# One PSUM read per engine for the transposed softmax weights of a query tile, kept in one tile per unit

## The chip, the cores and the metric

The kernel runs on one core of one Trainium2 chip. The metric is the device time of the whole program, in microseconds (us), as a median over several runs. Three runs of the kernel before gave 2176.07, 2176.35 and 2176.68 us.

## The reference, cut to what matters

The program computes sliding-window attention, then a feed-forward layer with a squared ReLU, then a dense mixture of eight experts with a Sinkhorn-normalised gate. Only the attention is touched:

```
B, H, S, D = 4, 8, 576, 64          # window 128
scores = scale * q @ k.T ; bias by distance ; masked outside 0 <= i - j < 128
attn = softmax(scores) ; attn_out = attn @ v
x = attn_out as (B*S, H*D) = (2304, 512)      # input of the feed-forward layer
```

With a window of 128, a tile of 128 queries sees at most two blocks of 128 keys: its own and the one before it.

## The kernel before

**Units.** The attention is cut into 32 units: four batches, two parts of a batch ("early": the query tiles 0, 1 and 2; "rest": the query tile 3 and a tail of 64 queries, numbered 4), and four pairs of heads. A unit loads k, q and v, transposes k and q on TensorE, and then works through its query tiles. Matmuls run on pairs of fp32r numbers: each operand is held as a rounded part (hi) and the remainder (lo), and a product is three matmuls, hi with hi, hi with lo and lo with hi. `split_ps` (L112) makes such a pair out of a PSUM tile: ScalarE (ACT) rounds PSUM into hi, then VectorE (DVE) subtracts hi from the same PSUM tile into lo.

**One query tile.** `attention_scores` (L257) computes the scores of two heads, the bias and the maximum, the exponential, the sum and the scaling, into the tile `s`. `attention_weights` (L302) transposes `s` with TensorE into one PSUM bank `pt` (L322: two heads by one or two key blocks, 128x128 each) and calls `split_ps` on it. Where a query tile has two key blocks, it calls it twice: first for the half of `pt` that belongs to the key block before, which goes into the second half of that block's tiles, then for the half of its own key block, which goes into the first half of new tiles. So there is one pair of tiles `p0`, `p1` for each key block, holding [head, own or next query tile, 128 queries]; three buffers of each stand in the pool (`weights`, L254). `attention_values` (L350) then multiplies by v: at query tile 1 it issues `block` (L327) for key block 0, at query tile 2 for key blocks 1 and 2, and in a rest unit, at the tail, for 3, 2 and 4. `block` is six matmuls into the PSUM tile `xo` (L336), whose first needs hi and whose second needs lo. `put_x` evicts `xo` into the input of the feed-forward layer.

**Order of the work.** `plan` (L375) lists steps: "q" for the transposes of k and q of a unit, "s" for the scores of a query tile, "t" for its weights and values. In the first four units two units alternate and "t" runs two steps behind "s"; after that one step behind. Before each of the five chunks of tokens of the feed-forward layer, `advance(needed(...))` makes sure that the attention of this chunk is done (L675), and inside a chunk `part` hands out the steps of the next chunk at three points of each of the 16 turns: after the first matmuls (h), in the middle of the second ones (acc), and at the end of the turn. The first chunk (384 tokens) also converts all weights from pairs of 32-bit words (`narrow`, L434: ACT L440 and L442, DVE L443, L444, L447 and L451, then the split in L453 and L454). Up to L720 the framework arranges each engine's queue: it takes the instructions in the order of the program, but lets a later one pass an earlier one that, by its own model of durations, isn't ready yet. From L720 on, the order of the program is kept.

Of the kernel before, what the change touches and what calls it, by code (L numbers as in the profile page):

```python
# [9 lines left out]
F32R = mybir.dt.float32r  # L10
# [13 lines left out]
def raw(ap):  # L24

    return ap.bitcast(F32)
# [3 lines left out]
def attention_moe_moe2(  # L30
# [12 lines left out]
    nc = tc.nc  # L43
    P = 128
# [7 lines left out]
    TAIL = S - FULL * P  # L52
# [26 lines left out]
    def chunk(c):  # L79
        return starts[c], widths[c]  # L80
# [13 lines left out]
    ident = const.tile([P, P], F32, name="ident")  # L94
# [17 lines left out]
    def split_ps(ps, hi, lo):  # L112
        nc.scalar.activation(hi, ps, AF.Copy)
        nc.vector.tensor_sub(lo, ps, raw(hi))
# [24 lines left out]
    ap = att.enter_context(tc.tile_pool(name="ap", bufs=1, side="right"))  # L139
# [22 lines left out]
    def at_ps(name, t, many=early):  # L162
        pool, tag = many[psn[0] % len(many)] if t["alone"] else (ps_at, "at")
        psn[0] += 1
        return pool.tile([P, 512], F32, name=name, tag=tag)
# [10 lines left out]
    def tails_ready():  # L176

        for i in range(SETS):
            for n in range(2):
                nc.scalar.activation(qtail[i][n].rearrange("p j c -> p (j c)"), ones, AF.Copy, scale=0.0)  # L180
        for hp in range(NPAIR):
            for j in range(2):
                nc.scalar.copy(
                    tbias[j * TAIL : (j + 1) * TAIL, hp, :], bias[0:TAIL, 2 * hp + j, : P + TAIL]
                )
# [19 lines left out]
    def attention_qk(n, t):  # L205

        rest = t["rest"]
        hi, lo = {}, {}
        for nm in "kq":
            hi[nm] = ap.tile([P, EARLY], F32R, name=f"{nm}h", tag=f"{nm}h", bufs=2)  # L210
            lo[nm] = ap.tile([P, EARLY], F32R, name=f"{nm}l", tag=f"{nm}l", bufs=2)
            t[nm + "h"], t[nm + "l"] = hi[nm], lo[nm]

        def turn(ps, nm, blocks, tail):
            o = 0
            for c in range(blocks + tail):
                rows = TAIL if c == blocks else P
                nc.tensor.transpose(
                    ps[:, o : o + rows], t[nm][:rows, c].rearrange("p j d -> p (j d)"), ident[:rows, :rows]
                )  # L220
                o += rows
            return ps[:, :o]

        if not rest:
            ps = turn(at_ps("tp_k", t), "k", 3, 0)
            split_ps(ps, hi["k"], lo["k"])
            ps = turn(at_ps("tp_q", t), "q", 3, 0)
            split_q(ps, hi["q"], lo["q"])
        else:
            both = at_ps("tp", t)  # L230
            ps = turn(both, "k", 2, 1)
            w = 2 * P + TAIL
            split_ps(ps, hi["k"][:, :w], lo["k"][:, :w])
            ps = turn(both[:, w:], "q", 1, 1)
            split_q(ps[:, :P], hi["q"][:, :P], lo["q"][:, :P])
            t["qt"] = qtail[n % SETS]
            for j in range(2):
                r = slice(j * D, (j + 1) * D)
                split_q(ps[r, P:], *[x[r, j, :] for x in t["qt"]])

    def attention_v(n, t):

        rest = t["rest"]
        vh, vl = t["vs"] = vsplit[n % SETS]
        cuts = [(slice(0, P), slice(0, 2)), (slice(0, TAIL), slice(2, 3))] if rest else [(slice(0, P), slice(0, 3))]
        for rows, ts in cuts:
            nc.scalar.activation(vh[rows, ts, ::2], t["v"][rows, ts], AF.Copy)
            nc.gpsimd.tensor_sub(vl[rows, ts, ::2], t["v"][rows, ts], raw(vh[rows, ts, ::2]))
# [3 lines left out]
        nc.vector.scalar_tensor_tensor(lo, ps, -(D ** -0.5), raw(hi), op0=ALU.mult, op1=ALU.subtract)  # L252

    def weights():  # L254
        return [ap.tile([P, 2, 2, P], F32R, name=f"p{n}", tag=f"p{n}", bufs=3) for n in range(2)]

    def attention_scores(hp, t, i):  # L257

# [43 lines left out]
    def attention_weights(t, i):  # L302

        s, tail, blocks = t[i], i == FULL, 2 if i else 1

        p = t["p"][i] = weights()
        if i and i - 1 not in t["p"]:
            t["p"][i - 1] = weights()
        pt = at_ps("pt", t)
        if tail:  # L310
            prev = t["p"][i - 1]
            for kb in range(2):
                nc.tensor.transpose(pt[:, kb * P : (kb + 1) * P], s[:, 0, kb * P : (kb + 1) * P], ident)
            pv = pt[:, :P].rearrange("p (j c) -> p j c", j=2)
            split_ps(pv, *[x[:, :, 1, :TAIL] for x in prev])
            pv = pt[:TAIL, P : 2 * P].rearrange("p (j c) -> p j c", j=2)
            split_ps(pv, *[x[:TAIL, :, 0, :TAIL] for x in p])
            return
        pv = pt.rearrange("p (a j c) -> p a j c", a=2, j=2)
        for j in range(2):  # L320
            for kb in range(blocks):
                nc.tensor.transpose(pv[:, kb, j, :], s[:, j, kb * P : (kb + 1) * P], ident)  # L322
        if i:
            split_ps(pv[:, 0], *[x[:, :, 1, :] for x in t["p"][i - 1]])
        split_ps(pv[:, blocks - 1], *[x[:, :, 0, :] for x in p])

    def block(t, kb, dst, a, w, first, last):  # L327

        rows = TAIL if kb == FULL else P
        vs = [x[:rows, kb - (2 if t["rest"] else 0)].rearrange("p a d -> p (a d)") for x in t["vs"]]  # L330
        n = 0
        for j in range(2):
            lh, ll = [x[:, j * D : j * D + P] for x in vs]
            rh, rl = [x[:rows, j].rearrange("p a c -> p (a c)")[:, a : a + w] for x in t["p"][kb]]
            for l, r in ((lh, rh), (lh, rl), (ll, rh)):
                nc.tensor.matmul(  # L336
                    dst, lhsT=l, rhs=r, start=first and n == 0, stop=last and n == 5, skip_group_check=True
                )
                n += 1
# [10 lines left out]
    def attention_values(b, hp, t, i):  # L350

        if i == 1:
            xo = t["xo"] = at_ps("xo", t, [xo_early[hp % 2]])
            block(t, 0, xo[:, : 2 * P], 0, 2 * P, True, False)
        if i == 2:
            xo = t["xo"]
            block(t, 1, xo[:, P : 3 * P], 0, 2 * P, False, False)
            block(t, 2, xo[:, 2 * P : 3 * P], 0, P, False, True)
            put_x(xo, hp, b * S, EARLY)
        if i == FULL:  # L360
            xo = at_ps("xo", t)
            block(t, 3, xo[:, : P + TAIL], 0, P + TAIL, True, False)
            block(t, 2, xo[:, :P], P, P, False, False)
            block(t, 4, xo[:, P : P + TAIL], 0, TAIL, False, True)
            put_x(xo, hp, b * S + EARLY, P + TAIL)
# [3 lines left out]
    ts = {}  # L369

    def load(n):
        if n < len(units):
            ts[n] = attention_load(*units[n])
# [33 lines left out]
    def advance(n):  # L407
        for kind, m, i in steps[done[0] : n]:
            b, hp, rest = units[m]
            if kind == "q":  # L410
                if m == NPAIR:
                    tails_ready()
                attention_qk(m, ts[m])
                ts[m]["p"] = {}
            elif kind == "s":
                attention_scores(hp, ts[m], i)
                if i in (1, FULL):
                    attention_v(m, ts[m])
                    load(m + 2)
            else:  # L420
                attention_weights(ts[m], i)
                attention_values(b, hp, ts[m], i)
        done[0] = max(done[0], n)
# [228 lines left out]
    def part(i):  # L652

        c, f = now
        if c < NCH - 1:
            a, b = [needed(starts[x] + widths[x]) for x in (c, c + 1)]
            advance(a + (b - a) * (3 * f + i) // (3 * NF1))
# [9 lines left out]
    for c in range(NCH):  # L667
        c0, n = chunk(c)
        if c == 1:
            cvs.close()  # L670
            xp2 = m1.enter_context(tc.tile_pool(name="xp2", bufs=1))
            for i in range(3, NCH):
                new_x(xp2, i)

        advance(needed(c0 + n))  # L675
        if c == NCH - 1:
            att.close()
# [6 lines left out]
        for f in range(NF1):  # L684
            now[:] = c, f
            a, bw = ahead.pop(0)
# [4 lines left out]
            hp, tag = (ps_mm, "mm") if c < NCH - 1 else (ps_at, "at")  # L691
# [14 lines left out]
            if len(pending) > LAG:  # L706
                t = pending.pop(0)
# [296 lines left out]
    for n in range(NP):  # L1004
        if n == 0:
# [16 lines left out]
            rh, rl = [x[:, 0, :HALF] for x in hidden[0]]  # L1022
# [243 lines left out]
```

## Time and profile before

| what | us |
|---|---|
| median of three runs | 2176.35 |
| span of the profiled execution | 2174.1 |
| median less the profiled span | 2.25 |
| DVE busy in 62 to 200 us of the span | 129.94 of 138 |
| PE busy in 200 to 602 us of the span | 397.88 of 402 |

Times inside the span are counted from its first instruction. PE is TensorE's matmul queue and PEld its queue of weight loads, which overlaps it. In a timeline row the first number is the start, the second the time taken, and the bracket says how long the engine had been idle and what released it. Instructions of one engine can overlap: a start can come before the end of the one in front. PEclk is the granted clock of TensorE as a share of full speed. The attention lies in the first 602 us; the experts fill the time from about 690 us on.

### The profile page before, as it was taken

What the parts mean: (1) busy time and instruction counts of PE and PEld (TensorE: products, weight loads), DVE (VectorE), ACT (ScalarE), POOL (GpSimd) and SP (SyncE); (2) the same over time, 40 slices, a digit from 0 to 9 for tenths busy, and PEclk for the clock granted to TensorE, in tenths of its full rate; (3) what the DMA queues carried; (4) which work ended last, traced back from release to release, by engine and by line L of the source; (5) the groups of instructions that cost most, each with busy time, mean ns of one, the idle gap of its engine ahead of it and who ended that gap; (6) DMA issues with size and microseconds to landing.
All of it is one profiled execution on the core that took longest, in us unless ns stands there. A gap on an engine that the chain in (4) does not pass through costs nothing.

```text
span 2174.1 us, 32629 instructions
## 1 busy us (share of the span) xinstructions
PE 2103.4 (97%) x11360; PEld 1925.0 (89%) x11360; DVE 1490.4 (69%) x2667; ACT 996.3 (46%) x2050; POOL 1070.5 (49%) x709
## 2 busy tenths in 40 slices
PE   6889999999999899999999999999999999999998
PEld 4778777777888788899999899999999999999998
DVE  7998455453244788887788677666778567777666
ACT  6776445443333444444444444444444544444443
POOL 2222223123254777788888544444546445454442
PEclk9899999999999999999999999999999999999999
DMA  6776545445475877687888988777777877778773
GB/s 186 219 246 209 148 148 162 143 148 177 157 259 170 300 276 294 263 331 284 320 287 299 333 275 265 260 260 260 259 260 265 271 260 252 253 258 269 259 260 125
DMA packets 281730, 525.49 MB, mean 242 GB/s; under 512 B 85584, under 2 KB 129760, under 8 KB 277472
## 3 DMA queue, kind: packets, MB, share of 16 engines
q1 hardware_dynamic: 281568, 523.42, 71.5%
q8 instruction: 91, 1.49, 0.3%
q14 instruction: 71, 0.58, 0.1%
HBM read 379.60 MB, written 143.73 MB: 241 GB/s over the span
## 4 chain that ended last, share of the span: by engine, by line
PE 77%; DVE 12%; ACT 3%; DMA 3%; issue 2%; POOL 1%; SPq 1%; ACTq 0%; POOLq 0%; DVEq 0%
PE y L119 9%; PE y L120 9%; PE y L118 9%; PE g L118 9%; PE g L120 9%; PE g L119 9%; PE h L118 3%; PE acc L118 3%; PE h L120 3%; PE h L119 3%; PE xo L336 3%; PE acc L120 3%; PE acc L119 2%; PE sc L282 2%; DVE rl L936 1%
## 5 line engine op out<-in xcount | busy, mean ns | idle before, releaser
L1086 POOL TENSOR_TENSOR rb<-R,rb 128x768 fp32r<-128x768 f32 x95 | 212.3, 2235 | 334.7 <-ACT rb L1081 322.3
L1117 DVE TENSOR_TENSOR a<-y,a 128x384 f32<-128x384 f32 x434 | 240.0, 554 | 180.0 <-PE y L120 178.0
L1086 POOL TENSOR_TENSOR rt<-R,rt 128x768 fp32r<-128x768 f32 x125 | 238.8, 1922 | 146.3 <-issue 61.7
L110 POOL TENSOR_TENSOR gl<-r,gh 128x512 fp32r<-128x512 f32 (+1 forms) x80 | 99.0, 1237 | 355.1 <-ACT gh L109 336.1
L110 POOL TENSOR_TENSOR w2a<-r,w2a 128x1024 fp32r<-128x1024 f32 x64 | 155.2, 2425 | 67.1 <-ACT w2a L109 67.1
L1081 ACT ACTIVATE rt<-R 128x768 fp32r<-128x768 f32 x128 | 107.7, 842 | 148.5 <-DVE R L1068 90.1
L118 PE MATMUL g<-xt,w1o 128*128 128x384 f32 x512 | 173.0, 338 | 0.9 <-ACT u L809 0.6
L120 PE MATMUL g<-xt,w1o 128*128 128x384 f32 x512 | 172.6, 337 | 0.0
L118 PE MATMUL y<-rt,w2o 128*128 128x384 f32 x512 | 172.4, 337 | 0.1
L120 PE MATMUL y<-rt,w2o 128*128 128x384 f32 x512 | 172.5, 337 | 0.0
L119 PE MATMUL g<-xt,w1o 128*128 128x384 f32 x512 | 172.4, 337 | 0.0
L119 PE MATMUL y<-rt,w2o 128*128 128x384 f32 x512 | 172.1, 336 | 0.0
L118 PE MATMUL y<-w2a,rh 128*128 128x512 f32 x384 | 151.1, 394 | 0.0
L119 PE MATMUL y<-w2a,rh 128*128 128x512 f32 x384 | 150.9, 393 | 0.2 <-POOL w2a L110 0.2
L120 PE MATMUL y<-w2a,rl 128*128 128x512 f32 x384 | 150.2, 391 | 0.0
L698 DVE SCALAR_TENSOR_TENSOR r<-h,r 128x512 f32<-128x512 f32 (+1 forms) x80 | 50.9, 636 | 134.5 <-ACT r L696 134.5
L1063 DVE TENSOR_TENSOR R<-R,pb 128x768 f32<-128x768 f32 x128 | 137.8, 1078 | 5.2 <-ACT R L1176 3.0
L118 PE MATMUL y<-rb,w2o 128*128 128x384 f32 x384 | 129.9, 338 | 2.8 <-DVE a L1117 2.1
L119 PE MATMUL y<-rb,w2o 128*128 128x384 f32 x384 | 130.0, 339 | 2.3 <-POOL rb L1086 2.3
L120 PE MATMUL y<-rb,w2o 128*128 128x384 f32 x384 | 129.9, 338 | 0.0
L120 PE MATMUL g<-xb,w1o 128*128 128x384 f32 x384 | 129.2, 336 | 0.0
L118 PE MATMUL g<-xb,w1o 128*128 128x384 f32 x384 | 129.1, 336 | 0.0
(231 smaller groups left out, 6234.4 us busy)
## 6 DMA issues: line engine op xcount, KB each, us to landing
w1o<-d_w SPq DMA_DIRECT2D x448, 256.0 KB, 3.1
w2o<-d_w SPq DMA_DIRECT2D x224, 512.0 KB, 4.0
d_w<-w1a SPq DMA_DIRECT2D x32, 1792.0 KB, 11.7
d_w<-w2a SPq DMA_DIRECT2D x32, 1536.0 KB, 8.1
a<-d_in SPq DMA_DIRECT2D x64, 512.0 KB, 3.8
b<-d_out SPq DMA_DIRECT2D x64, 512.0 KB, 3.6
r<-in_moe_w_dram SPq DMA_DIRECT2D x64, 512.0 KB, 4.3
u<-in_moe_w_in_dram SPq DMA_DIRECT2D x16, 512.0 KB, 4.6
```

Of the source, the lines that this page charges most:

```text
L110: (eng or nc.gpsimd).tensor_sub(lo, src, raw(hi))
L118: nc.tensor.matmul(ps, lhsT=lh, rhs=rh, start=first, stop=False, **kw)
L119: nc.tensor.matmul(ps, lhsT=lh, rhs=rl, start=False, stop=False, **kw)
L120: nc.tensor.matmul(ps, lhsT=ll, rhs=rh, start=False, stop=last, **kw)
L282: nc.tensor.matmul(sc[:, :nk], lhsT=lhs, rhs=rhs, start=x == 0, stop=x == 2)
L336: nc.tensor.matmul(dst, lhsT=l, rhs=r, start=first and n == 0, stop=last and n == 5, skip_group_check=True)
L698: nc.vector.scalar_tensor_tensor(g[:, :n], ph[:, :n], 0.0, r[:, :n], op0=ALU.max, op1=ALU.mult)
L936: nc.vector.scalar_tensor_tensor(rl, src, 0.0, raw(rh), op0=ALU.max, op1=ALU.subtract)
L1063: nc.vector.tensor_mul(r, r, pb[:, None, :].to_broadcast([P, 2, HALF]))
L1081: nc.scalar.activation(x[:, 0], R[m, f, h], AF.Copy)
L1086: eng.tensor_sub(x[:, 1], R[m, f, h], raw(x[:, 0]))
L1117: nc.vector.tensor_add(acc[dst][:, dt], ps[:, :HALF], acc[dst][:, dt])
```

## The change

A unit now has one pair of tiles `p0`, `p1` for all its key blocks, with six columns of 128 per head, and two buffers each. Key block k of the unit owns the columns 2k (own queries) and 2k + 1 (the next query tile), so what a query tile needs to write for the block before and for its own block lies side by side. The transposes write `pt` as [head, key block, queries], and one `split_ps` covers both key blocks. Of the tail, whose key blocks have 128 and 64 rows, the two calls stay. `block` takes its columns from the common tile.

```diff
     def weights():
-        return [ap.tile([P, 2, 2, P], F32R, name=f"p{n}", tag=f"p{n}", bufs=3) for n in range(2)]
+        return [ap.tile([P, 2, 6 * P], F32R, name=f"p{n}", tag=f"p{n}", bufs=2) for n in range(2)]
...
-        p = t["p"][i] = weights()
-        if i and i - 1 not in t["p"]:
-            t["p"][i - 1] = weights()
+        if not t["p"]:
+            t["p"] = weights()
+        kb0 = 2 if t["rest"] else 0
+        at = max(0, 2 * (i - kb0) - 1) * P
         pt = at_ps("pt", t)
         if tail:
-            prev = t["p"][i - 1]
             for kb in range(2):
                 nc.tensor.transpose(pt[:, kb * P : (kb + 1) * P], s[:, 0, kb * P : (kb + 1) * P], ident)
-            pv = pt[:, :P].rearrange("p (j c) -> p j c", j=2)
-            split_ps(pv, *[x[:, :, 1, :TAIL] for x in prev])
-            pv = pt[:TAIL, P : 2 * P].rearrange("p (j c) -> p j c", j=2)
-            split_ps(pv, *[x[:TAIL, :, 0, :TAIL] for x in p])
+            for kb, rows in ((0, P), (1, TAIL)):
+                pv = pt[:rows, kb * P : (kb + 1) * P].rearrange("p (j c) -> p j c", j=2)
+                split_ps(pv, *[x[:rows, :, at + kb * P : at + kb * P + TAIL] for x in t["p"]])
             return
-        pv = pt.rearrange("p (a j c) -> p a j c", a=2, j=2)
+        pv = pt[:, : 2 * blocks * P].rearrange("p (j c) -> p j c", j=2)
         for j in range(2):
             for kb in range(blocks):
-                nc.tensor.transpose(pv[:, kb, j, :], s[:, j, kb * P : (kb + 1) * P], ident)
-        if i:
-            split_ps(pv[:, 0], *[x[:, :, 1, :] for x in t["p"][i - 1]])
-        split_ps(pv[:, blocks - 1], *[x[:, :, 0, :] for x in p])
+                nc.tensor.transpose(pv[:, j, kb * P : (kb + 1) * P], s[:, j, kb * P : (kb + 1) * P], ident)
+        split_ps(pv, *[x[:, :, at : at + blocks * P] for x in t["p"]])
...
     def block(t, kb, dst, a, w, first, last):
         rows = TAIL if kb == FULL else P
-        vs = [x[:rows, kb - (2 if t["rest"] else 0)].rearrange("p a d -> p (a d)") for x in t["vs"]]
+        kb -= 2 if t["rest"] else 0
+        vs = [x[:rows, kb].rearrange("p a d -> p (a d)") for x in t["vs"]]
+        a += 2 * kb * P
...
-            rh, rl = [x[:rows, j].rearrange("p a c -> p (a c)")[:, a : a + w] for x in t["p"][kb]]
+            rh, rl = [x[:rows, j, a : a + w] for x in t["p"]]
...
-                ts[m]["p"] = {}
+                ts[m]["p"] = None
```

## Rows read from the trace of the kernel before

**Rows 1.** Busy us of each engine by stage of the span (stage, length, engines, clock, DMA).
```profile
20.00:62.00 42.00, 34.28 (x182) 27.21 (x182) 36.17 (x134) 29.73 (x92) 4.33 (x6) 0.92 0.55 171
62.00:200.00 138.00, 126.33 (x706) 108.03 (x705) 129.94 (x367) 98.08 (x259) 33.29 (x32) 0.94 0.74 232
200.00:602.00 402.00, 397.88 (x2066) 310.26 (x2066) 174.18 (x590) 173.63 (x492) 97.60 (x101) 0.99 0.52 158
690.00:2174.10 1484.10, 1452.71 (x7907) 1394.05 (x7906) 1105.92 (x1495) 649.81 (x1114) 886.21 (x513) 0.99 0.78 269
```

**Rows 2.** Waits by total (us, times, longest): DVE in 62:200, DVE in 20:62, PE in 200:602.
```profile
DVE b L454 <- ACT b L453: 2.0, 4, 0.7
...
DVE p L114 <- ACT p L113: 4.5, 5, 1.8
...
PE xo L336 <- DVE p L114: 3.1, 4, 0.8
PE xo L336 <- ACT p L113: 0.7, 3, 0.3
```

**Rows 3.** The tile p by stage, 20:62, 62:200, 200:602: the DVE subtractions into it.
```profile
L114 DVE TENSOR_TENSOR p<-pt,p x20: 401/421/425, 26.6 to 59.2; 128x256 fp32r<-128x256 f32 x20
...
L114 DVE TENSOR_TENSOR p<-pt,p x34: 263/410/425, 74.7 to 198.7; 128x256 fp32r<-128x256 f32 x26, 128x128 fp32r<-128x128 f32 x4, 64x128 fp32r<-64x128 f32 x4
...
L114 DVE TENSOR_TENSOR p<-pt,p x90: 270/418/426, 201.7 to 599.9; 128x256 fp32r<-128x256 f32 x66, 128x128 fp32r<-128x128 f32 x12, 64x128 fp32r<-64x128 f32 x12
```

**Rows 4.** Groups by shape in 0:620, DVE then ACT: busy us, mean ns, idle before.
```profile
L114 DVE TENSOR_TENSOR p<-pt,p 128x256 fp32r<-128x256 f32 x112 | 46.9, 419 | 23.8 <-ACT p L113 23.6
...
L114 DVE TENSOR_TENSOR xl<-acc,xh 128x512 fp32r<-128x512 f32 x12 | 7.6, 682 | 0.8 <-ACT xh L113 0.8
...
L113 ACT ACTIVATE p<-pt 128x256 fp32r<-128x256 f32 x112 | 42.1, 377 | 31.2 <-PE pt L322 17.3 <-DVE p L114 13.6
...
L113 ACT ACTIVATE xh<-acc 128x512 fp32r<-128x512 f32 x12 | 6.5, 590 | 0.1
```

**Rows 5.** Timeline of DVE: starts behind a 256-wide and behind a 512-wide PSUM read.
```profile
28.23 0.42 DVE L114 TENSOR_TENSOR p<-pt,p 128x256 fp32r<-128x256 f32 x1
28.56 0.41 DVE L285 CUSTOM_DVE_ANT_0 s<-sc,bias 128x256 f32<-128x256 f32 x1
...
211.94 0.69 DVE L698 SCALAR_TENSOR_TENSOR r<-h,r 128x512 f32<-128x512 f32 x1 [1.13 <-ACT r L696]
212.54 0.41 DVE L285 CUSTOM_DVE_ANT_0 s<-sc,bias 128x256 f32<-128x256 f32 x1
```

**Rows 6.** Timeline: the two evictions of one query tile, query tile 3 of a rest unit.
```profile
208.69 0.38 ACT L113 ACTIVATE p<-pt 128x256 fp32r<-128x256 f32 x1
...
209.50 0.43 DVE L114 TENSOR_TENSOR p<-pt,p 128x256 fp32r<-128x256 f32 x1
...
209.96 0.38 ACT L113 ACTIVATE p<-pt 128x256 fp32r<-128x256 f32 x1 [0.89 <-DVE p L114]
...
210.38 0.43 DVE L114 TENSOR_TENSOR p<-pt,p 128x256 fp32r<-128x256 f32 x1 [0.45 <-ACT p L113]
```

**Rows 7.** Timeline of PE: matmuls around the first two of xo in one tail.
```profile
259.53 0.36 PE L336 MATMUL xo<-p,vsplit 128*128 128x192 f32 x1 [0.28 <-ACT p L113]
259.72 0.41 PE L120 MATMUL acc<-gh,b 128*128 128x512 f32 x1
260.90 1.33 PE L336 MATMUL xo<-p,vsplit 128*128 128x192 f32 x10 [0.76 <-DVE p L114]
```

**Rows 8.** Busy us and clock in short stretches behind two xo groups (columns as rows 1).
```profile
262.00:266.00 4.00, 4.00 (x20) 2.89 (x19) 0.44 (x2) 0.74 (x2) 1.00 (x1) 0.59 0.06 7
266.00:270.00 4.00, 4.00 (x11) 3.14 (x12) 1.65 (x8) 1.09 (x4) 0.00 (x0) 0.56 0.57 173
...
409.00:412.00 3.00, 3.00 (x12) 2.01 (x12) 1.14 (x5) 1.06 (x3) 1.00 (x1) 0.58 0.21 55
```

## The prediction

> **What bounds the kernel now.** I read the busy time by stage first, since each engine's share of the whole span mixes stages with different limits. The attention lies in the first 602 us, in three stages. From 20 to 62 us (the first four units) DVE is busy 36.17 of 42 us and PE 34.28: neither is full, and chains between engines set the time. From 62 to 200 us, while the weights are also converted, DVE is busy 129.94 of 138 us: DVE is the bound, and PE has slack. From 200 to 602 us PE is busy 397.88 of 402 us, and DVE and ACT under half. Behind 690 us no weights of the attention are touched [rows 1]. So the question is what the edit takes off DVE before 200 us, and whether it moves PE's 4.1 us of idle time after it.
>
> Then the waits. In 62 to 200 us DVE's longest wait by total is 2.0 us and is for another split: no wait for the rounding of p has a row there. In 20 to 62 us DVE waits 4.5 us for ACT's p, five times. In 200 to 602 us PE's idle time before xo is 3.1 us for DVE's p and 0.7 us for ACT's [rows 2].
>
> **What goes: 48 roundings and 48 subtractions.** An early unit has two query tiles with two key blocks and a rest unit one, so 16 x 2 + 16 x 1 = 48 pairs of evictions become 48 single ones. The subtractions of 256 columns say where. An early unit has one that stays alone, so in 20 to 62 us it is (20 - 4)/2 = 8 pairs; in 62 to 200 us, with four early units begun, (26 - 4)/2 = 11; after 200 us, with eight, (66 - 8)/2 = 29 [rows 3].
>
> **What one pair is worth to DVE.** 419 ns become 682 ns, the duration of the same instruction on 512 columns: 2 x 419 - 682 = 156 ns by durations. But DVE overlaps: behind a 256-wide subtraction the next instruction starts after 0.33 us, behind a 512-wide PSUM read after 0.60 us [rows 4, 5]. Where DVE is full, a pair is worth 2 x 0.33 - 0.60 = 0.06 to 0.07 us. I take 0.07.
>
> The Trainium skill, "VectorE: DVE Perf Modes", section "The DRAIN you can't avoid", says that the next instruction does not start until the pipe has emptied, and that one that isn't held starts earlier. By the first half a pair would be worth the whole 156 ns; the row shows the next start 0.09 us before the end, so the second half holds here. With the first half, the term for 62 to 200 us below would be 1.7 us in place of 0.8.
>
> **62 to 200 us.** 11 x 0.07 = 0.8 us of DVE time. DVE is the bound, so I count it in full; the ends are 0 (the chain passes elsewhere) and 11 x 0.156 = 1.7 us. ACT loses about as much (2 x 377 - 590 = 164 ns a pair [rows 4]) at 98.08 of 138 us busy [rows 1]: worth nothing by itself, as ACT's work lies beside DVE's; if DVE's cover were gone, at most 11 x 0.164 = 1.8 us.
>
> **20 to 62 us.** Here a chain counts. Both evictions of a query tile read one bank, and they run one behind the other: ACT from 208.69, DVE from 209.50, ACT again from 209.96, released by DVE, DVE again until 210.81, that is 2.12 us [rows 6]. The merged pair takes 0.59 + 0.68 = 1.27 us: the last weight is there 0.85 us earlier. Two units alternate, so eight pairs make four rounds, and the upper end is 4 x 0.85 = 3.4 us. The other end is a loss: where DVE already waits for the first rounding (five times [rows 2]), this is 590 - 377 = 213 ns later, 1.1 us in all. Between them I take 1.1 us of gain: 8 x 0.07 = 0.6 us, because DVE is 86% busy there and so nearer to the stage that follows, and 0.5 us for the chain.
>
> **200 to 602 us.** PE is full, so what DVE and ACT save (29 pairs) is worth nothing; their work lies beside the feed-forward matmuls. What can move is PE's idle time before xo, 3.8 us. In query tile 2 the last weights come earlier. But the first key block of query tile 1 or 2 needed only the first eviction; now its first matmul waits 213 ns longer, and its second, which needs lo, (590 + 682) - (377 + 419) = 476 ns longer [rows 4]. Behind that matmul stand all later ones of PE's queue. The queue's planner fills such gaps with feed-forward matmuls, as one acc matmul between the first and second of xo shows [rows 7]. Ends: a gain of 3.8 us plus the clock's dips below, and a loss that I price as a rival. I take 0.4 us of gain, because the present waits are short and few (seven), and the longer first eviction offsets most of the shorter last one.
>
> **At nothing.** The transposes keep number and size; the columns that `block` reads are contiguous before and after; the tail keeps two evictions; no DMA is issued, dropped or moved. The tiles take 24 KB a partition in place of 12, which issues nothing. A unit's tiles now wait for the unit two before it, where a key block's tiles waited for the block three before: looser, and no row shows a wait for it. One tile for all blocks could make an eviction wait for the xo matmuls of the query tile before; these have been issued a step earlier. If that cover is gone, the price is a group of xo matmuls ahead of ACT.
>
> **The sum.** 0.8 + 1.1 + 0.4 = 2.3 us off the profiled span of 2174.1 us gives 2171.8. The median of the runs is 2.25 us over that span, and I keep that distance: 2174.0 us, 0.11% less. A change under 0.2% (4.35 us) can't be told from none here.
>
> **Rival A, faster: PE's hiccups go with the chain.** Twice in 200 to 602 us TensorE falls to about half its clock (0.59 and 0.56 over 8 us, 0.58 over 3 us), the first time just after xo had been held up by p for 0.28 and 0.76 us [rows 7, 8]. At full clock these stretches would be shorter by 4 x 0.41 + 4 x 0.44 + 3 x 0.42 = 4.7 us. If shorter evictions remove both, the sum is 2.3 + 4.7 = 7.0 us: 2169.3. For it speaks that the idle time named p; against it, that this xo group belongs to a tail, whose two evictions stay. Chance 0.25.
>
> **Rival B, slower: the first key block waits for the whole eviction.** From 200 us on, eight early units have two such starts each: 16 x 0.476 = 7.6 us of PE time, where PE is the bound. It decides where the planner leaves less than 1.27 us of other matmuls between transposes and xo. For it: PE already waited seven times. Against it: these matmuls are there at every step, and the planner's model lengthens the eviction too. Less the gains of the first two stages, 2176.35 + 7.6 - 1.9 = 2182.1; at half exposure 2178.3. Chance 0.13.
>
> **Rival C, slower: another order of the queues.** The planner orders everything up to 602 us anew, and PE can stall and lose its clock at other units: two more stretches like that at 262 us (3.5 us each) give 2174.0 + 7.0 = 2181.0. For it: it takes only a stall of about 1 us [rows 7]. Against it: before, only two groups of many met it. Chance 0.10.
>
> **How the numbers follow.** The forecast has 0.52; of that 0.10 lies past 0.2% faster, 0.41 within and 0.01 slower. Rival A is all faster (0.25). Rival B gives 0.04 within and 0.09 slower, C 0.02 within and 0.08 slower. Together faster 0.35, within 0.47, slower 0.18. The forecast's own range is 2171 to 2177. For 8 in 10 I go down past rival A to 2167 (the upper ends of the first two stages, 1.7 + 3.4, and the dips, 4.7, would give 2166.6) and up to 2181, where most of B and C lies inside.
>
> **What would show it.** Right: 112 subtractions of 128x256 become 16, beside 48 of 128x512 at about 680 ns; the stage up to 200 us shorter by about 2 us with DVE still near 94% busy; from there to the end of the attention the same length within 1 us. Wrong: more than 2 us of PE idle added before xo, waiting for p (B); a low clock at another unit (C); both dips gone (A); or a stage up to 200 us that gains over 4 us, by which the chain of evictions, and not DVE's time, would have been the limit.

## The result, and the profile after

The changed kernel takes 2188.05 us, the median of five runs (2181.93 to 2196.44), beside 2176.35 us of the kernel before (2175.17 to 2177.53) on the same chip: a ratio of 1.0054, 95% interval 1.0033 to 1.0075. It is slower by about 0.5%. Five later sets of runs each had the kernel before on the same chip; three of them timed the changed kernel again and gave 1.0027, 1.0052 and 1.0038. So the sign is sure, and the size lies between 0.3 and 0.5%. The profiled execution took 2187.84 us, with a span of 2186.1 us.

The evictions did become what the diff says. Groups by shape in 0 to 620 us of the changed kernel (busy us, mean ns, idle before), against [rows 4]:

```profile
L114 DVE TENSOR_TENSOR p<-pt,p 128x512 fp32r<-128x512 f32 x48 | 33.0, 687 | 12.6 <-ACT p L113 12.3
L114 DVE TENSOR_TENSOR p<-pt,p 128x256 fp32r<-128x256 f32 x16 | 6.6, 413 | 0.2
...
L113 ACT ACTIVATE p<-pt 128x512 fp32r<-128x512 f32 x48 | 28.4, 591 | 17.4 <-PE pt L321 17.3
L113 ACT ACTIVATE p<-pt 128x256 fp32r<-128x256 f32 x16 | 6.0, 376 | 1.4 <-PE pt L321 1.1
```

112 subtractions of 256 columns became 16, beside 48 of 512, at 687 ns (forecast 682) and 591 ns for the rounding (590). DVE spends 46.9 - 39.6 = 7.3 us less on them. The time was not lost in the instructions themselves.

By stage, the columns as in [rows 1] (the stages of the changed kernel end up to 10 us later, so the windows are not the same work):

```profile
20.00:62.00 42.00, 34.94 (x134) 27.06 (x135) 31.18 (x118) 25.96 (x74) 2.01 (x2) 1.00 0.54 164
62.00:200.00 138.00, 125.89 (x697) 109.42 (x697) 125.17 (x343) 96.87 (x242) 31.46 (x32) 0.90 0.71 220
200.00:602.00 402.00, 397.84 (x2084) 308.94 (x2085) 176.70 (x582) 173.50 (x475) 99.25 (x104) 1.00 0.53 159
```

The first row holds the news: in 20 to 62 us TensorE issued 134 matmuls where it had issued 182 [rows 1], yet it was busy as long, 34.94 against 34.28 us. It ran at its lower pace. The clock column shows 1.00 there, but the profile has no record of the clock before the first change; the pace of the matmuls shows the level: four transposes (pt) take 1.12 us at 30.27 us, and 0.60 us once the clock is up.

Because the windows hold different work, I measured the same work in every profile instead, between two starts that all have. Stretch A runs from the first xo matmul to the feed-forward layer's first matmul (h), and covers the first four units; stretch C runs from the r of the second chunk's first turn (r is ACT's output behind h, one in each turn) to that of the fifth chunk, and lies in 200 to 602 us. What the recorded texts call the first expert matmul, slice or pass is the feed-forward layer's. "Low" is the time in C at the lower clock, "rise" the first record at which TensorE's clock goes up, 1.2 to 2.4 GHz. The kernels of the table are described in the next section.

| kernel (profiled run) | merged where | rise, us | A, us | C, us | low in C, us |
|---|---|---|---|---|---|
| before | nowhere | 34.0 | 30.27 | 398.33 | 10.2 |
| e1_two | nowhere | 37.0 | 29.60 | 395.56 | 3.4 |
| f2_before_x2 | nowhere | 33.6 | 29.69 | 395.71 | 3.4 |
| k2_before_hold | nowhere | 38.7 | 29.37 | 393.53 | 0 |
| e2_late | later units | 34.0 | 30.15 | 401.30 | 13.7 |
| h3_late2 | later units | 36.3 | 30.50 | 396.62 | 3.4 |
| e3_early | first four | 34.4 | 32.95 | 393.55 | 0 |
| e7_early2 | first four | 34.9 | 32.91 | 397.94 | 10.2 |
| l1_after | all | 32.9 | 32.17 | 395.13 | 0 |
| l3_after | all | 32.6 | 32.59 | 401.31 | 13.7 |
| l4_after | all | 35.8 | 33.62 | 395.08 | 0 |
| f1_after_x2 | all | 34.0 | 32.48 | 395.65 | 0 |
| after | all | 62.9 | 37.87 | 395.08 | 0 |
| l2_after | all | 65.6 | 38.58 | 395.13 | 0 |

Three things stand in this table. A is 29.4 to 30.5 us without merged evictions in the first four units and 32.2 to 33.6 us with them, when the clock rises early: means 29.9 and 32.8, **2.9 us more**. Where the clock rises late, A is 38 us. And C, at an equal low time, is 0.9 to 1.6 us longer with merged later units: 395.1 to 395.7 against 393.5 at no low time (**1.6 us**, f1 with its other change left out), 396.6 against 395.6 and 395.7 at 3.4 us.

### The profile page after: what moved, and what is told of

It reads as the page before. It is cut to its first block, busy times and chain, and to the rows that moved or that the text cites. A ratio compares the mean times of both kernels' runs of the same rounds, so it can differ in the third digit from the quotient of the medians.

```text
span 2186.1 us, 32509 instructions
## 1 busy us (share of the span) xinstructions
PE 2113.4 (97%) x11360; PEld 1932.6 (88%) x11360; DVE 1483.1 (68%) x2619; ACT 993.4 (45%) x2002; POOL 1068.4 (49%) x709
## 4 chain that ended last, share of the span: by engine, by line
PE 79%; DVE 10%; ACT 3%; DMA 3%; issue 2%; POOL 2%; SPq 1%; ACTq 0%; POOLq 0%; DVEq 0%
PE y L119 9%; PE y L118 9%; PE y L120 9%; PE g L118 9%; PE g L120 9%; PE g L119 9%; PE xo L335 3%; PE h L118 3%; PE h L119 3%; PE acc L118 3%; PE h L120 3%; PE acc L120 3%; PE acc L119 2%; PE sc L282 2%; PE pt L321 1%
```

## The experiments

Five sets, each on one chip with runs of the kernel before. "After" is the changed kernel.

**e1_two: the new tiles, but two evictions again.**

```diff
-        split_ps(pv, *[x[:, :, at : at + blocks * P] for x in t["p"]])
+        for kb in range(blocks):
+            c = slice(kb * P, (kb + 1) * P)
+            split_ps(pv[:, :, c], *[x[:, :, at + kb * P : at + (kb + 1) * P] for x in t["p"]])
```

> The new layout (one tile per unit, transposes ordered by head) with two evictions per query tile again. Theory 1 (TensorE's clock: in the changed kernel it is first raised at 62.9 us and not at 34.0, and the stage up to 64 us takes 9 us more for it): the time follows the first rise of the clock; a rise near 34 us gives 2173 to 2179 us, a late one 2183 to 2196. Theory 2 (the merged eviction holds up the first key block, whatever the clock): within 3 us of the kernel before, 2173 to 2179. Theory 3 (one tile per unit reorders the queues, and the merge itself costs nothing): as slow as the changed kernel, 2184 to 2192.

Measured 2178.88 us, ratio 1.0010 (0.9999 to 1.0021). Tiles, transposes' columns and buffers cost nothing that can be told from none here, at most 0.21%; most of the loss is in the merged evictions.

**e2_late and h3_late2 (the same kernel on another chip): merged everywhere but in the first four units.**

```diff
+        if t["alone"]:      # the first four units
+            for kb in range(blocks): ...   # two evictions, as in e1_two
+        else:
             split_ps(pv, *[x[:, :, at : at + blocks * P] for x in t["p"]])
```

> Merged evictions everywhere but in the first four units, which evict in two. Theory 1: the first rise of the clock comes back to about 34 us, the first ACT rounding of r to about 64 us, the time 2170 to 2178. Theory 2: the first stage is as before, but the later 40 merges each hold up xo, 2178 to 2186. Theory 3: 2184 to 2192.

> The merged evictions in all units but the first four, a second time, as the yardstick of this set: no xo wait over 0.2 us before the first r, the first r at 64 to 65 us, the wait acc<-POOL gl at the end of the first expert pass at 0.8 to 2 us, and 0.999 to 1.002 of the kernel before if both of the first result's places of loss (the first four units, the end of the first pass) are absent in it.

Measured 1.0006 (0.9994 to 1.0019) and 1.0000 (0.9988 to 1.0012). 40 of the 48 pairs are merged here, and the kernel stands level with the one before. The end of the feed-forward layer's fourth chunk (the "first expert pass" of the recorded texts) was not as expected in h3: the wait acc<-POOL gl was 2.9 us, and that handover (from the r of the fifth chunk's first turn to that of its ninth) took 44.24 us where the same program had taken 41.41 in e2.

**e3_early and e7_early2 (again the same kernel): merged in the first four units alone.** The condition above is turned round.

> Merged evictions in the first four units alone (8 pairs), two evictions in all others. All three theories put the loss where these are: 2183 to 2192. If the later 40 merges had a share, 2178 to 2182. Theory 1 adds that the first rise comes past 45 us when the time is long.

> The merged evictions in the first four units alone, a second time. If these eight pairs cost what the profile of the first such run shows (the first r 4.4 us later, of which 2.0 us are TensorE's waits for the whole eviction), 1.001 to 1.003 of the kernel before. If the late first rise of the clock belongs to them too, some of the single times lie 8 to 10 us over the others and a profile may show a rise at 63 us or later; if it needs the merged evictions of the later units as well, none does.

Measured 1.0013 (0.9999 to 1.0027) and 1.0026 (1.0013 to 1.0038): eight merged pairs cost more than the other forty (the intervals of h3 and e7 lie just apart, those of e2 and e3 overlap). Neither profile had a late rise.

**e4_warm and e5_before_warm: 60 unread matmuls of 128x256 in the first two units**, in after and in before, to keep TensorE at work early.

```diff
                 attention_scores(hp, ts[m], i)
+                if (m, i) in ((0, 0), (1, 0), (1, 1)):
+                    wt = ps_acc.tile([P, 512], F32, name="wt", tag="acc")
+                    k = ts[m]["kh"]
+                    for _ in range(12 if i else 24):
+                        nc.tensor.matmul(wt[:, : 2 * P], lhsT=k[:, :P], rhs=k[:, P : 3 * P], start=True, stop=True)
```

> The changed kernel with 60 more matmuls (128x256, results unread) put between the first scores of the first two units, where TensorE has idle time. Theory 1: the clock rises before 25 us, the first ACT rounding of r comes near 64 us in place of 73.8, and the time falls to 2172 to 2180 with a smaller spread between runs. Theories 2 and 3: the chains don't depend on the clock, the first rounding of r stays past 72 us and the time stays at 2184 to 2192 or above, by up to 4 us for the added matmuls.

> The same 60 matmuls in the kernel before. Theory 1: its clock rises earlier than 34 us as well, worth 0 to 4 us: 2172 to 2177. Theories 2 and 3: no gain, 2176 to 2180 for the added matmuls.

Measured 1.0041 (1.0024 to 1.0058) and 1.0003 (0.9993 to 1.0012). The clock rose at 15.2 and 15.3 us, and fell again before 30 us in both. After stays slower than before by as much as without the matmuls, so the late rise is not all of the loss: A took 32.06 us, with 27.60 in e5.

**e6_fill: 96 unread matmuls of 128x128** into columns of xo that nobody reads, 12 ahead of the values of the query tiles 1 and 2 in the first four units.

> The changed kernel with 12 more small matmuls (128x128, into columns of xo that nothing reads) behind the transposes of each query tile with two key blocks of the first four units, 96 in all, where TensorE waits for the merged eviction. Theory 1: TensorE is busier there, the first rise comes before 45 us, the first rounding of r by 68 us, the time 2174 to 2182. Theories 2 and 3: no gain, 2184 to 2194.

Measured 1.0110 (1.0094 to 1.0127), with the first rise at 74.3 us, the latest of all. More matmuls in this stretch did not bring an earlier rise, so my idea that idle gaps of TensorE keep its clock down fell.

**l1_after, l2_after, l3_after, l4_after: after itself, four more times.**

> The changed kernel once more, timed beside the others of this study, with a second profile. Theory 1 (the clock's first rise decides): the time differs from run to run with the rise; where this profile's rise comes before 45 us its first ACT rounding of r is before 68 us and the time below 2184, where it comes past 55 us the time is 2185 to 2196. Theory 2 (the first key block waits for the whole eviction, whatever the clock) and theory 3 (the order of the queues): the first rounding of r stays past 71 us whenever the rise comes, median 2184 to 2192.

> A third profile of the changed kernel, for the spread of the first rise of the clock (34.0 us in the kernel before, 37.0 and 34.0 in the two kernels that evict in two in the first units, 62.9 in the changed kernel). Theory 1: a rise past 45 us again in most profiles of this kernel. Theories 2 and 3: the rise is a matter of chance and comes at 30 to 40 us in this one, with the first rounding of r past 71 us all the same.

> The changed kernel once more, as the yardstick of this set. If the loss is the kernel's and not one chip's, 1.002 to 1.006 of the kernel before again. The single times fall into two groups if the clock's first rise comes early in some executions and late in others: about 2176 to 2183 with a first rise near 33 us, 2187 and over with one near 63 to 66 us.

> The changed kernel, the yardstick of this set: 17 conversions in the stretch, 32.2 to 33.0 us of it with an early rise of the clock and 35 us or more with a late one, and 1.002 to 1.006 of the kernel before.

Measured 1.0027 (1.0011 to 1.0044), one execution of 2189.04 us, 1.0052 (1.0036 to 1.0068) and 1.0038 (1.0022 to 1.0053). The first rise came at 32.9, 65.6, 32.6 and 35.8 us. The executions did not fall into two clean groups as I had expected: l3 rose early in its profile, and its six times lay at 2183.99 to 2193.92.

**f1_after_x2 and f2_before_x2: two buffers for x2**, GpSimd's sum that the DMA takes out, here at the end of the feed-forward layer's fourth chunk.

```diff
-                x = rp.tile([P, CH], F32, name="x2", tag="x2", bufs=1)
+                x = rp.tile([P, CH], F32, name="x2", tag="x2", bufs=2)
```

> The changed kernel, with two buffers instead of one for x2, the sum that GpSimd writes at the end of the first expert pass and that the DMA takes out, so that the next sum doesn't wait for the DMA before. Theory 1: a part of the change's loss comes at 625 to 640 us, where the first expert pass ends: GpSimd's x waits 3.4 us for d_x<-x there (2.4 us before the change), the expert stage behind it starts late and TensorE's clock is lowered for 6.8 us. Without the wait the 4.1 us lost there fall to 0 to 1.5: 2 to 4 us under the changed kernel of the same set (about 2178 against 2181), and no wait x<-DMA d_x over 0.5 us. Theory 2: the wait is beside the path (the late event is the weight split xt<-q on GpSimd ahead of it): the stretch stays 3 to 4 us longer than before the change, and the time stays within 1.5 us of the changed kernel.

> The kernel before, with two buffers instead of one for x2: the control of the run above. Theory 1 (the wait costs only where it falls late, as in the changed kernel): 0 to 1 us under the kernel before, 1.000 of it. Theory 2 (two buffers are worth something in any order): as much as in the run above, 2 to 4 us under it.

Measured 1.0050 (1.0036 to 1.0065) and 1.0038 (1.0023 to 1.0053). The wait x<-DMA d_x went (0.5 us in f1, none named in f2), and nothing was gained. For the changed kernel that is theory 2: f1 took 2186.17 us beside 2187.37 of l3, and its stretch stayed long. For the kernel before both theories fell: it became slower. The timeline of POOL in f2 (start, length) shows what followed:

```profile
617.21 2.90 POOL L507 TENSOR_TENSOR x<-xh,xl 128x512 f32<-128x512 f32 x2
620.07 2.17 POOL L110 TENSOR_TENSOR w1a<-r,w1a 128x512 fp32r<-128x512 f32 x2
...
625.77 1.25 POOL L507 TENSOR_TENSOR x<-xh,xl 128x512 f32<-128x512 f32 x1
626.99 1.94 POOL L110 TENSOR_TENSOR gl<-r,gh 128x384 fp32r<-128x384 f32 x2
```

Two sums x stand back to back ahead of the weights' split, and the last one ahead of gl, the operand that TensorE waits for. TensorE's wait in that handover, in before and then in f2:

```profile
PE acc L119 <- POOL gl L110: 1.9, 1, 1.9
```

```profile
PE acc L119 <- POOL gl L110: 3.6, 1, 3.6
```

It seems that the wait of x for the DMA had kept its place in the queue for others; that this is the whole of f2's loss is not shown, since k2, with one buffer, has as long a handover. After waits 2.9 us here, and its profile loses 4.1 us in this handover. Whether that is the change's stays open. The same handover is 41.4 to 41.7 us in before and in the profiles of e1, e2, e3, e5 and e6, and 43.2 to 46.1 us in all others, with the layout of before (f2, k2) as with the new one, and for one program both ways (e2 and h3, e3 and e7). But all five profiles of after itself are long, 43.9 to 46.0 us, and the one of before is short, 41.6.

**h1_sub2 and h2_act2: after, with only the subtraction (h1) or only the rounding (h2) split in two in the first four units.**

```diff
+        if t["alone"]:
+            nc.scalar.activation(hi, pv, AF.Copy)
+            for kb in range(blocks):
+                c = slice(kb * P, (kb + 1) * P)
+                nc.vector.tensor_sub(lo[:, :, c], pv[:, :, c], raw(hi[:, :, c]))
+        else:
+            split_ps(pv, hi, lo)
```

> The changed kernel, with the subtraction of a pair split in two again in the first four units alone; the rounding stays one instruction. Theory 1 (the first key block's matmuls wait for the whole merged eviction in these units): up to the first r TensorE's wait xo<-DVE p, 1.0 us in every profile with merged early evictions and an early rise of the clock, falls to 0.2 or less, xo<-ACT p stays at 0.6 to 1.0, and the first r comes about 1 us earlier than the changed kernel's 66.6 to 68.5, the time 1.003 to 1.005 of the kernel before. Theory 2 (the wait is of no weight; the later start of the first expert slice, h<-xl 2.0 us against 1.1, and the order of the turns behind it carry the loss): both xo waits change but the first r stays at 67 to 69 us.

> The same with the rounding split in two in the first four units and the subtraction merged. Theory 1: xo<-ACT p, 0.6 to 1.0 us, falls to 0.2 or less, xo<-DVE p stays near 1.0 us or grows; the first r comes up to 1 us earlier than in the changed kernel. Theory 2: the first r stays at 67 to 69 us.

Measured 1.0027 (1.0014 to 1.0040) and 1.0010 (0.9998 to 1.0022). In h2 the waits moved as theory 1 said: xo<-ACT p is gone and xo<-DVE p is 0.9 us. In h1 xo<-DVE p is gone and xo<-ACT p is 0.4, but h1 had a late rise (62.1 us), and after and l2, whose rise is late too, have the same two values without any split, so h1 shows nothing on this wait. The first r came at 72.58 us in h1 and at 68.00 in h2, no earlier than after's. The intervals overlap; this pair does not settle which half costs more.

**k1_after_hold and k2_before_hold: the loads of the weight slices 6, 7 and 8 are held** until the first, third and fourth input of the first chunk is written, by a one-element copy into their tile.

```diff
             words[i] = cv.tile([P, DM, 2], U32, name="u", tag="u", bufs=3)
+            if i in (6, 7, 8):
+                nc.gpsimd.tensor_copy(words[i][:1, 0, :1].bitcast(F32), raw(xl[0][:1, (0, 2, 3)[i - 6], :1]))
```

> The changed kernel, with the loads of the weight slices 6, 7 and 8 held until the first, third and fourth input of the first chunk is written (GpSimd copies one element of it into the slice's tile ahead of the load). Theory 1 (conversions pulled forward): with merged evictions the framework puts more of the weight conversion on VectorE into the first four units, 17 instructions of 10.4 to 11.2 us between the first xo matmul and the first expert matmul in place of 10 of 5.9, and TensorE waits for p behind them. Held back, there are at most 12 of them (about 7 us), that stretch falls from 32.2 to 33.0 us (at an early rise of the clock) to 30 to 31, and the time to 1.000 to 1.003 of the kernel before, 2 us or more under the changed kernel of this set. Theory 2 (the merged eviction itself makes the stretch long, by its own longer wait): the conversions leave but the stretch stays at 32 us or more, and the time within 1.5 us of the changed kernel's.

> The kernel before with the same three loads held: the control. Its conversions in the first four units are few already (10 instructions), so theory 1 expects 8 to 10 of them, the stretch at 29.6 to 30.5 us, and 0.999 to 1.002 of the kernel before. A gain of more than 0.2% here would say that late loads are worth something by themselves, a loss that the run above has to be read against it.

Measured 1.0023 (1.0008 to 1.0038) and 0.9982 (0.9970 to 0.9993), beside 1.0038 of after in this set. The hold gives 0.18% in the kernel before. In the changed kernel the gain is not clear: 0.15% by the ratios, whose intervals overlap, and none by the medians (2183.73 and, for l4, 2183.57 us). So it is not the cure of this change: the two layouts stay 0.4% apart with it. In k1, 13 conversions of 8.6 us stayed in A, not at most 12, and A fell only to 31.69 us. k2, the kernel before with the hold, at 2172.83 us, beats both kernels.

## Why the prediction was wrong

I forecast 2174.0 us in a range of 2167 to 2181; it is 2188.05. By the steps:

**What one pair is worth to DVE: right.** Behind the 512-wide subtraction the next DVE instruction starts 0.60 us later (the rows from 299.67 us below), as taken. The first half of what I had weighed of the Trainium skill ("VectorE: DVE Perf Modes", section "The DRAIN you can't avoid"), that the pipe empties before the next instruction starts, is again not what the rows show: the start comes 0.08 us before the end. They agree with its second half, that a next instruction that is not held starts earlier.

**20 to 62 us: this step failed, with its sign.** I took 1.1 us of gain, between a gain of 3.4 and a loss of 1.1; A is 2.9 us longer. The chain that I counted on did get shorter: from the first rounding to the last subtraction a pair took 2.7 us in before and takes 1.6 in l3 (means of the eight pairs, taken in the order of the queues). TensorE gained nothing from it.

Nor is it, in the main, the clock that makes A longer. In four of the six profiles without merging here (before, f2, e2 and h3) TensorE is busy 26.6 to 27.3 us of A and idle 2.9 to 3.2; in five of the six with it (e3, e7, l1, l3 and f1) it is as busy, 26.9 to 27.3 us, and idle 5.2 to 6.1. The lower clock behind the rise did last longer, 10.2 to 10.4 us against 6.8, but that does not show in the busy time. In l4 it does: 13.7 us of it, 29.8 us busy and 3.9 idle. (Left out: e1 and k2, whose rise came later, with 1.4 to 1.5 us idle and 27.9 to 28.1 busy.)

Two things that I had written down for other places happen here, and each makes a wait. The first is rival B's mechanism. In the tile before, the first key block's matmuls could start after the first of two evictions. Now they wait for the whole one, and in the first four units little else stands in TensorE's queue. TensorE's waits in A up to the start of h (us, times, longest), before and then l3_after, whose A starts at the same time as before's within 0.22 us:

```profile
PE pt L322 <- DVE s L299: 2.1, 1, 2.1
PE sc L282 <- DVE p L114: 0.2, 1, 0.2
PE pt L322 <- DVE p L114: 0.2, 1, 0.2
```

```profile
PE h L118 <- DVE xl L114: 2.0, 1, 2.0
PE pt L321 <- DVE s L299: 1.4, 1, 1.4
PE xo L335 <- DVE p L114: 1.0, 1, 1.0
PE xo L335 <- ACT p L113: 0.9, 3, 0.5
```

Before the change, xo never waits for p here; after it, 1.9 us in four waits. The timeline of l3 shows the two longest, with the wait in brackets:

```profile
34.37 0.39 PE L335 MATMUL xo<-p,vsplit 128*128 128x256 f32 x1 [0.47 <-ACT p L113]
...
43.76 1.46 PE L335 MATMUL xo<-p,vsplit 128*128 128x256 f32 x11 [1.01 <-DVE p L114]
```

Waits of xo for p of 1.6 to 2.0 us stand in every profile with the whole pair merged in these units and an early rise (e3, e7, l1, l3, l4, f1), and at most 0.2 us in the six of the table without merging here (e5, with its matmuls for the clock, has 0.9). Where the rise is late, they are 0.4 us. I had priced rival B "from 200 us on" alone, where its cover is best, and left out the stage without cover.

The second is rival C's, another order of the queues, and it makes the longest wait of all: 2.0 us of h for xl, the input of the feed-forward layer. The timeline of DVE in l3:

```profile
60.36 0.68 DVE L446 SCALAR_TENSOR_TENSOR cv<-u,cv 128x512 uint32<-128x512 uint32 x1
60.97 0.41 DVE L443 TENSOR_SCALAR cv<-cv 128x512 uint32<-128x512 uint32 x1
61.30 0.94 DVE L450 CUSTOM_DVE_ANT_0 cv<-cv,cv 128x1024 uint16<-128x1024 uint16 x1
62.16 0.55 DVE L114 TENSOR_TENSOR xl<-xo,xh 128x384 fp32r<-128x384 f32 x1
```

ACT has its half of this input, xh, at 61.40 us, but DVE has just begun one more weight conversion, and h starts at 62.76. This wait is 1.8 to 2.0 us in all eight profiles of the table with merging here. Without it h starts at once (k2: 0.3 us) and waits 0.7 to 1.2 us for the next xl, just behind A. Up to the first r, then, the stretch is 2.6 us longer in place of 2.9, and in the nine profiles above 1.0 us of that is busy time (in l3 the clock falls again at 63.3 us, just behind A). The window A of before and of l3 (length, then busy us of PE, PEld, DVE, ACT and POOL with counts, clock, DMA):

```profile
29.95:60.22 30.27, 27.33 (x156) 22.04 (x156) 25.04 (x97) 20.42 (x66) 3.08 (x3) 0.89 0.39 107
```

```profile
30.17:62.76 32.59, 27.28 (x155) 22.23 (x155) 29.37 (x97) 22.06 (x62) 4.30 (x5) 0.84 0.46 130
```

DVE has 97 instructions in both, but is busy 4.3 us longer. Eight subtractions fewer made room for weight conversions from later, as the groups of A show, before and then l3:

```profile
L451 DVE CUSTOM_DVE_ANT_0 cv<-cv,cv 128x1024 uint16<-128x1024 uint16 x2 | 1.5, 734 | 0.0
L447 DVE SCALAR_TENSOR_TENSOR cv<-u,cv 128x512 uint32<-128x512 uint32 x2 | 1.4, 689 | 0.0
L444 DVE TENSOR_SCALAR cv<-cv 128x512 uint32<-128x512 uint32 x2 | 0.8, 423 | 0.0
```

```profile
L450 DVE CUSTOM_DVE_ANT_0 cv<-cv,cv 128x1024 uint16<-128x1024 uint16 x3 | 3.1, 1026 | 0.0
L446 DVE SCALAR_TENSOR_TENSOR cv<-u,cv 128x512 uint32<-128x512 uint32 x4 | 2.8, 696 | 0.0
L443 DVE TENSOR_SCALAR cv<-cv 128x512 uint32<-128x512 uint32 x4 | 2.2, 554 | 0.0
```

In all, 17 conversions of 10.2 to 11.1 us stand in A where there were 10 of 5.8 to 5.9. The number follows the subtraction: 16 in h2, where only the rounding is split, and 10 again in h1, where the subtraction is. So the relief that I counted as a gain was spent at once on work that is due later, ahead of evictions that are due now. The hold took four of these away: in k1 the wait of h for xl is 0.3 us and A is 31.69 us, against 33.62 in l4, whose low stretch is as long; the 1.6 us for p stayed. So both waits belong to the 2.9 us. How much of it each makes is not shown: other waits moved too (pt for s fell by 0.7 us in l3), A holds 149 matmuls in k1 and 155 in l4, and h1, with its 10 conversions, still measured 1.0027.

**The late rise: no step held it.** In four of the twelve profiles with merged evictions, whole or half, in the first four units (after, l2, h1 and e6; e4, with its matmuls for the clock, left out) TensorE's clock went up at 62 us or later. In the six without (before, e1, e2, h3, f2 and k2; e5 left out likewise) it never did. By these numbers that can be chance. Two windows of before, then of after, with the columns as above:

```profile
40.00:50.00 10.00, 7.61 (x47) 5.77 (x46) 8.45 (x35) 7.80 (x25) 2.01 (x2) 0.88 0.52 177
50.00:60.00 10.00, 9.76 (x54) 8.09 (x54) 7.19 (x25) 5.96 (x19) 1.07 (x1) 0.77 0.21 45
```

```profile
40.00:50.00 10.00, 9.93 (x45) 7.46 (x44) 6.94 (x28) 5.40 (x17) 1.01 (x1) 1.00 0.47 130
50.00:60.00 10.00, 10.00 (x39) 8.00 (x38) 5.94 (x23) 5.71 (x18) 1.00 (x1) 1.00 0.32 101
```

After is busy all the time and issues fewer matmuls. The same program, with the same queues, has A at 32.2 to 33.6 us when the clock rises early and at 37.9 and 38.6 when it rises late: 5 us. What decides between the two stays open.

**62 to 200 us: not decided.** The forecast gain of 0.8 us is smaller than what the clock does there: this stage, from the first r to that of the second chunk, took 141.43 us in before, 140.92 in e1 and 140.67 in h2, each with 17.1 us at the lower clock, and 142.1 in after with 23.9.

**200 to 602 us: the sign was wrong.** I took 0.4 us of gain, out of the idle time before xo; at no low time C is 1.6 us longer, and the idle time did not shrink. C in e3 and then in l1, both at no low time (columns as in [rows 1]):

```profile
207.81:601.36 393.55, 389.60 (x2044) 304.22 (x2044) 171.50 (x578) 170.63 (x481) 96.62 (x99) 1.00 0.50 159
209.77:604.90 395.13, 391.00 (x2044) 303.44 (x2044) 167.78 (x550) 167.35 (x453) 96.48 (x99) 1.00 0.50 158
```

TensorE waits 3.7 us for p before xo in e3 and 3.9 in l1, where rival B had priced 7.6 us more; 1.4 of the 1.6 us are busy time, of as many matmuls. By the starts of r the loss stands where early units pass: the six turns from 293.84 us in e3 take 1.1 us longer in l1 and those from 436.80 us 1.0, and all others together 0.5 less. In such a unit the first key block does wait for the whole eviction. The timeline of TensorE in e3, where this unit has two evictions:

```profile
295.73 0.60 PE L321 MATMUL pt<-ident,s 128*128 128x128 f32 x4
...
297.13 0.39 PE L339 MATMUL xo<-p,vsplit 128*128 128x256 f32 x1
...
297.81 0.84 PE L339 MATMUL xo<-p,vsplit 128*128 128x256 f32 x5
```

and of the same unit in l1_after, with ACT and DVE:

```profile
297.40 0.60 PE L321 MATMUL pt<-ident,s 128*128 128x128 f32 x4
...
299.03 0.39 PE L335 MATMUL xo<-p,vsplit 128*128 128x256 f32 x1
...
300.40 0.85 PE L335 MATMUL xo<-p,vsplit 128*128 128x256 f32 x5 [0.28 <-DVE p L114]
...
298.40 0.58 ACT L113 ACTIVATE p<-pt 128x512 fp32r<-128x512 f32 x1
...
299.67 0.68 DVE L114 TENSOR_TENSOR p<-pt,p 128x512 fp32r<-128x512 f32 x1
300.27 0.28 DVE L285 CUSTOM_DVE_ANT_0 s<-sc,bias 128x128 f32<-128x128 f32 x1
```

From the transposes to the second xo matmul it takes 297.81 - 295.73 = 2.08 us with two evictions and 3.00 with one. The planner fills most of this with acc and sc matmuls; 0.28 us is left as a wait. So what I had put against rival B here, that other matmuls are there at every step, held: of its 7.6 us at most 1.6 came. How the delay becomes busy time is not shown; the order of the matmuls changed as well, and the profile models their ends, so short waits can hide in busy time.

**Rivals A and C: the dips' price was right, the mechanism wrong.** The two dips of before [rows 8] are absent in after's profile:

```profile
262.00:270.00 8.00, 7.66 (x39) 5.50 (x37) 3.27 (x14) 3.31 (x10) 2.03 (x2) 1.00 0.76 229
409.00:412.00 3.00, 3.00 (x18) 2.16 (x17) 1.11 (x5) 1.17 (x3) 0.00 (x0) 1.00 0.49 171
```

C without low time and without merging is 393.5 us, 4.8 us less than before's 398.33; I had priced the dips at 4.7. But they come and go without the change: k2, with the old tiles, has none, though TensorE's waits for p before xo are the same 3.7 us there as in e1 with one dip, and l3, with the new ones, has both:

```profile
268.00:275.00 7.00, 7.00 (x23) 5.19 (x23) 2.08 (x9) 1.83 (x6) 1.01 (x1) 0.51 0.36 103
414.90:421.70 6.80, 6.80 (x22) 4.99 (x22) 2.09 (x9) 1.83 (x6) 1.01 (x1) 0.50 0.38 106
```

**At nothing: right** within what e1 can tell (1.0010, at most 1.0021).

**The sum.** 2.9 us of A and 1.6 of C make 4.5 us, 0.21%. The sets measured 0.27 to 0.54%. The late rise, 5 us in some executions, lies on top. The rest, one to some us, I can't assign. The largest candidate is the handover from the fourth chunk to the fifth, 2.3 to 4.4 us longer in the five profiles of after than in before's; the clock's other dips move by as much between executions of one program.

## What to carry to other kernels

Merging two evictions into one saves engine time, but it delays the first consumer until the second half is done; price this at the place with the least other work for the waiting engine, here the start, and not at the steady stage alone. Where a planner orders the queues, time freed on an engine can be refilled at once with work that is due later, so look at what moves into the gap and at who waits behind it: the longest new wait here was not for the merged tile at all. Compare stretches of equal work, and at equal clock, before a difference of two spans is explained: here one profile gained 4.8 us from two dips that the change had not touched.

## What the hardware showed that I had not expected

- One program rose to its higher clock at 32.6 to 35.8 us in three profiles and at 62.9 and 65.6 in two. With 96 more matmuls (e6) it was 74.3 us in one profile.
- The lower clock has a steady price in C: with merged later units 395.1 to 395.7 us at no low time, 396.6 at 3.4 us and 401.3 at 13.7.
- With a wait for a DMA gone (f2), the kernel before lost 0.4%: GpSimd then did its sums ahead of the operand that TensorE was waiting for, and that wait grew from 1.9 to 3.6 us.
